# One row of branch B's output weights in three transfers instead of one: a gated pair of attention decodes

## The chip, the core and the metric

The kernel runs on one core of a Trainium2 chip. The metric is the device time of one execution in microseconds; it is taken from several runs, and one execution was profiled beside them. The core has a tensor engine (PE), a vector engine (DVE), a scalar engine (ACT), GpSimd (POOL) and a queue engine (SP, SyncE) that issues most of the transfers. Sixteen DMA engines carry every transfer between HBM and the on-chip buffers.

## The reference

Two branches, A and B, each decode one token for two sequences with 32 heads of 128 over a cache of 4096 tokens. All data are float32.

```python
def branch(x, k_cache, v_cache, wq, wo):          # x: 2 x 1 x 512
    q = (x @ wq).reshape(B, 1, 32, 128).transpose(0, 2, 1, 3)
    scores = einsum("bhqd,bhkd->bhqk", q, k_cache) * 128 ** -0.5
    p = softmax(scores)
    o = einsum("bhqk,bhkd->bhqd", p, v_cache)
    return o.transpose(0, 2, 1, 3).reshape(B, 1, 4096) @ wo     # wo: 4096 x 512

g = sigmoid((A_x * gate_w).sum(-1, keepdims=True))
out = g * branch(A_x, A_k, A_v, A_wq, A_wo) + (1 - g) * branch(A_x, B_k, B_v, B_wq, B_wo)
```

Each of the four caches has 134 MB and each of the four weight matrices 8.4 MB; every byte is read once.

## The kernel before

The work is cut into 32 units: a branch, a group of four heads, and a sequence. A unit's K and its V are 8.4 MB each, laid out as 128 partitions of 64 KB. Three buffers of that size exist: `kt[0]` and `kt[1]` for K in turn, and `vt` for V. DVE multiplies K by the query and sums (L392, L395), takes the maxima, ACT makes the exponentials, and PE multiplies them with V (L371).

SP issues nearly all loads, in the order in which the program is written, and waits before each until its buffer is free. At the end of its list stand the V of the last unit (`load_v(NU - 1)`, into `kt[0]`), branch A's output weights (`load_wo("A")`, into `vt`) and branch B's (`load_wo("B")`, into `kt[1]`, once DVE has read the last K there).

Output weights lie as 128 partitions of 32 rows (`OR` = 32), each row 512 numbers, 2 KB. `load_wo("B")` brings them in seven transfers, each with a semaphore of its own (slots `a`, `b`, `c`, `h`, `i`, `j`, `k`): rows 0 to 15, 16 to 23, 24 to 27 (`EARLY` is 28), 28 and 29, 30, and the two halves of row 31. `load_parts` issues a transfer for each pair of cuts and keeps, in `parts`, what to wait for. PE consumes rows in order: `project_out` multiplies rows 0 to 27 into the accumulator `most` (L466) and waits at the first row of each part; `project_last` multiplies rows 28 to 31 in four strips (L481), with one wait for each part. Between them ACT copies `most` to `kept` (L582), and four small matmuls fold it in (L586). DVE and ACT then copy the four strips to the on-chip totals (L597, L596), and SP and ACT each store one half of the output.

Of the kernel before, what the change touches and what calls it, by code (L numbers as in the profile page):

```python
# [12 lines left out]
P = 128  # L13
# [15 lines left out]
OR = H * DH // P  # L29
DQ = DH // OR  # L30
EARLY = OR - 4
PAD = 72
NP = 2 * NG
SCALE = DH ** -0.5
# [13 lines left out]
class Streams:  # L48
# [32 lines left out]
    def put(self, e, make, reads=(), writes=(), gives=None):  # L81

        self.before(e, reads, writes)
        i = make(self.engines[e])
        if gives is not None:
            i.then_inc(gives, 1)
            return None
        self.ticks[e] += 1
        i.then_inc(self.sems[e], 1)
        point = self.sems[e], self.ticks[e]  # L90
        self.after(point, reads, writes)
        return point
# [51 lines left out]
def tile_gated_decode(ctx: ExitStack, tc: tile.TileContext, ins: dict, out: bass.AP):  # L144
# [12 lines left out]
    slot = small.tile([P, VC], F32, name="slot")  # L157
# [12 lines left out]
    ones = small.tile([P, 1], F32, name="ones")  # L170
    small.tile([P, PAD], F32, name="pad")
    kt = [big.tile([P, NS, DH], F32, name=f"kt{i}") for i in range(2)]
# [9 lines left out]
    with tc.tile_critical():  # L182
        S = Streams(nc, tc)
# [25 lines left out]
        parts = {}  # L209

        def load_parts(item, t, src, slots, *cuts):
            parts[item] = [S.dma("sp", t[:, i:j], src[:, i:j], slot=s) for s, i, j in zip(slots, cuts, cuts[1:])]

        def arrived(e, item, *which):
            p = parts[item]
            S.wait(e, [p[k] for k in which] if which else p)
# [27 lines left out]
        def load_wo(n):  # L244
            t = wo[n]
            src = ins[n + "_wo"].rearrange("(p r) e -> p r e", p=P)
            if n == "A":
                nc.sync.wait_ge(v_free, NU - 1)
                load_parts(("wo", n), t, src, "f", 0, OR)
                return  # L250
            nc.sync.wait_ge(k_free[1], NU // 2)
            load_parts(("wo", n), t, src, "abchi", 0, OR // 2, 3 * OR // 4, EARLY, OR - 2, OR - 1)
            parts["wo", n] += [S.dma("sp", t[:, OR - 1, h], src[:, OR - 1, h], slot=s) for s, h in zip("jk", HALVES)]

        wo = {n: t.rearrange("p r d -> p (r d)").rearrange("p (r e) -> p r e", e=D) for n, t in (("A", vt), ("B", kt[1]))}

# [13 lines left out]
        def vput(e, make, reads=(), writes=(), **kw):  # L270
# [6 lines left out]
                                     slot="y"))  # L277
# [180 lines left out]


        def project_out(k, n, *rows_):  # L460
            bounds = (0,) if n == "A" else (0, OR // 2, 3 * OR // 4)
            for r in range(*rows_):
                if r in bounds:
                    arrived("pe", ("wo", n), bounds.index(r))
                s = r % STRIPS
                put("pe", lambda x: x.matmul(most[s * QT:s * QT + B], on[:, k, r], wo[n][:, r],  # L466
                                             start=n == "A" and r < STRIPS, stop=n == "B" and r >= EARLY - STRIPS),
                    [r_on], [r_most])
# [5 lines left out]
        def strips(*which):  # L474
            for s in which or range(STRIPS):
                yield s, r_acc[s], acc[s][s * QT:s * QT + B, :W], slice(s * W, (s + 1) * W)

        def project_last(part, r, *which):
            arrived("pe", ("wo", "B"), part)
            for _, a, t, e_ in strips(*which):  # L480
                put("pe", lambda x: x.matmul(t, on[:, 1, r], wo["B"][:, r, e_], start=r == EARLY, stop=r == OR - 1), [r_on], [a])  # L481

# [26 lines left out]
        for u in range(2, NU):  # L509
            load_k(u)  # L510
            load_v(u - 1)
        load_v(NU - 1)
        load_wo("A")
        load_wo("B")

        exps(0, 0, 0, lambda make, gives: put("act", make, [r_nm[0], r_sc, r_pad, r_lp, r_nil], [], gives))
# [61 lines left out]
        r_on.writers = [point]  # L578

        project_out(0, "A", OR)  # L580
        project_out(1, "B", EARLY)
        put("act", lambda x: x.activation(kept, most, AF.Copy), [r_most], [r_kept])  # L582
        for r in range(EARLY, OR - 2):
            project_last(3, r)
        for _, a, t, e_ in strips():
            put("pe", lambda x: x.matmul(t, fold, kept[:, e_], start=False, stop=False), [r_fold, r_kept], [a])  # L586
        project_last(4, OR - 2)
        project_last(5, OR - 1, 0, 1)
        project_last(6, OR - 1, 2, 3)

        for h, e in enumerate(("sp", "act")):
            r_total = [R(), R()]
            for i in range(2):
                _, a, t, _ = next(strips(2 * h + i))
# [27 lines left out]
```

## Time and profile before

| | |
|---|---|
| median of 3 runs | 1324.02 us (1323.88 to 1324.05) |
| the profiled execution | 1324.03 us |
| its span, first to last instruction | 1322.2 us |
| DVE busy | 1165.2 us (88%) |
| PE busy | 333.5 us (25%) |
| ACT busy | 100.7 us (8%) |
| DMA | 570.51 MB, mean 431 GB/s over the span |

The profiled execution agrees with the median of the runs. The span is what the trace covers; the rest of the execution lies before the first and after the last instruction. Busy shares are averages over the whole span. The DMA share that the profile gives is the mean over sixteen DMA engines, so a share of 0.125 is two engines at work.

### The profile page before, as it was taken

To read this page: it belongs to the slowest core of one execution; us is meant where nothing else is said; L and a number is where in the kernel's file an instruction comes from. 1 tells how busy PE (TensorE), PEld (TensorE's weight loads), DVE (VectorE), ACT (ScalarE), POOL (GpSimd) and SP (SyncE) were. 2 spreads that over 40 slices of the span, in tenths; PEclk is the share of its full clock that TensorE was granted. 3 is DMA by queue.
4 is the path that set the end of the run, shared out by engine and by line. 5 is a ranking of instruction groups with operands and counts; after the bars stand their busy time and mean duration, and the time that the engine had idled before them with its cause. 6 is when DMAs were issued, how large, how long until landed. Compare 5 with 4: busy or idle time off the path is not lost. (4 is left out here: it accounts for less than half of the span.)

```text
span 1322.2 us, 6170 instructions
## 1 busy us (share of the span) xinstructions
PE 333.5 (25%) x2358; PEld 90.2 (7%) x2358; DVE 1165.2 (88%) x316; ACT 100.7 (8%) x328; POOL 0.7 (0%) x6
## 2 busy tenths in 40 slices
PE   3112223211222221122222122222212232221255
PEld 0000000000000000000000000000000000000011
DVE  1988999999999999999999999999999999999961
ACT  0000100001010000101000010100001010000100
POOL 0000000000000000000000000000000000000000
PEclk9566666556666655666665566666556666655678
DMA  9999999999999999999999999999999999999998
GB/s 406 451 412 443 442 418 442 440 428 432 442 432 426 442 440 418 442 442 416 442 442 418 442 442 428 430 442 434 424 442 442 416 442 442 416 442 442 423 438 350
DMA packets 10820, 570.51 MB, mean 431 GB/s; under 512 B 1207, under 2 KB 1467, under 8 KB 1726
## 3 DMA queue, kind: packets, MB, share of 16 engines
q1 hardware_dynamic: 10804, 570.43, 99.6%
q8 instruction: 3, 0.05, 0.0%
q14 instruction: 3, 0.02, 0.0%
q10 hardware_dynamic: 10, 0.01, 0.0%
HBM read 570.43 MB, written 0.00 MB: 431 GB/s over the span
## 5 line engine op out<-in xcount | busy, mean ns | idle before, releaser
L392 DVE TENSOR_TENSOR kt<-kt,q 128x16384 f32<-128x16384 f32 x31 | 534.0, 17225 | 70.6 <-DVEq L97 70.6
L395 DVE TENSOR_REDUCE sc<-kt 128x128 f32<-128x16384 f32 x31 | 533.8, 17220 | 1.1
L371 PE MATMUL vp<-vt,pr 128*32 128x512 f32 x1984 | 285.0, 739 | 913.5 <-PEq L97 913.5
L371 PEld LDWEIGHTS vp<-vt,pr 128*32 128x32 f32 x1984 | 78.3, 133 | 1120.2 <-issue 1120.2
L367 ACT ACTIVATE pr<-sc,nm 32x128 f32<-32x128 f32 x128 | 50.9, 398 | 107.0 <-ACTq L97 101.7
L430 ACT ACTIVATE pr<-nil 128x512 f32<-128x512 f32 x31 | 19.3, 623 | 457.4 <-ACTq L97 457.4
L451 ACT ACTIVATE vs<-vp,slot 128x128 f32 x15 | 5.5, 367 | 448.6 <-ACTq L97 448.6
L337 PE MATMUL qa<-vt,cols 128*2 128x512 f32 x128 | 19.1, 764 | 39.3 <-PEq L97 39.3
L367 ACT ACTIVATION_READ_ACCUMULATOR pr<-sc,nm (+1 forms) x128 | 23.5, 184 | 0.0
L416 DVE SCALAR_TENSOR_TENSOR vs<-vp,slot,vs 128x128 f32 x45 | 15.8, 351 | 8.6 <-DVEq L97 7.6
L597 DVE COPY kt<-qa 2x128 f32<-2x128 f32 x1 | 0.3, 278 | 23.6 <-PE qa L481 23.6
L352 DVE STREAM_TRANSPOSE vt<-vt 128x1024 f32<-128x1024 f32 x2 | 2.5, 1225 | 17.2 <-ACT vt L348 17.2
L498 DVE TENSOR_REDUCE sc<-kt 128x64 f32<-128x8192 f32 x2 | 17.4, 8686 | 0.1
L496 DVE TENSOR_TENSOR kt<-kt,q 128x8192 f32<-128x8192 f32 x2 | 17.4, 8686 | 0.0
L455 ACT ACTIVATE vp<-nil 128x512 f32<-128x512 f32 x15 | 9.0, 600 | 98.5 <-ACTq L97 98.5
L544 DVE SCALAR_TENSOR_TENSOR vs<-vp,slot,vs 128x128 f32<-128x128 f32 x3 | 1.1, 351 | 13.4 <-ACT vs L542 13.3
L371 PE MATMUL vp<-kt,pr 128*32 128x512 f32 x64 | 9.5, 759 | 10.4 <-DMA kt<-in_B_v_cache_dram 10.4
L400 DVE TENSOR_REDUCE rm<-sc 128x1 f32<-128x128 f32 x31 | 8.7, 281 | 2.3
L406 DVE STREAM_TRANSPOSE q<-qsel 128x128 f32<-128x128 f32 x30 | 9.3, 311 | 1.0
L466 PE MATMUL most<-vt,kt 128*2 128x512 f32 x64 | 8.4, 684 | 6.0 <-DMA vt<-in_A_wo_dram 6.0
L289 DVE COPY cols<-bank 128x8 f32<-128x8 f32 x1 | 0.2, 166 | 10.2 <-PE bank L287 10.2
L401 DVE STREAM_TRANSPOSE across<-rm 128x32 f32<-128x32 f32 x31 | 6.6, 212 | 1.1
(73 smaller groups left out, 56.7 us busy)
## 6 DMA issues: line engine op xcount, KB each, us to landing
kt<-in_A_k_cache_dram SPq DMA_DIRECT2D x2, 4096.0 KB, 35.6
kt<-in_B_wo_dram SPq DMA_DIRECT2D x1, 4096.0 KB, 33.3
kt<-in_B_wo_dram SPq DMA_DIRECT2D x1, 2048.0 KB, 37.7
kt<-in_B_wo_dram SPq DMA_DIRECT2D x1, 1024.0 KB, 39.7
kt<-in_B_wo_dram SPq DMA_DIRECT2D x1, 512.0 KB, 40.5
vt<-in_A_v_cache_dram SPq DMA_DIRECT2D x16, 28.3
kt<-in_B_k_cache_dram SPq DMA_DIRECT2D x16, 42.6
kt<-in_B_wo_dram SPq DMA_DIRECT2D x1, 256.0 KB, 40.6
```

What stands on the lines that cost most here:

```text
L337: last = nc.tensor.matmul(t[h * QT:h * QT + B], cols[:, c], blocks[:, c, i, h], start=c == 0, stop=c == KC - 1)
L367: do(lambda x: x.activation(padded[h, :, b, j * VC:(j + 1) * VC], s[h].rearrange("p (c a) -> p c a", a=VC), AF.Exp, bias=m[h], accum_out=l ...
L371: return x.matmul(vp[c % STRIPS * QT:(c % STRIPS + 1) * QT], padded[:, c].rearrange("p b m -> p (b m)"), t[:, c * VC:(c + 1) * VC].rearran ...
L392: at = D_.do(lambda x: x.tensor_tensor(kt[o], kt[o], q[:, None, :].to_broadcast([P, NS, DH]), op=ALU.mult), after)
L395: at = D_.do(lambda x: x.tensor_reduce(sc[o], kt[o], axis=AX.X, op=ALU.add), at)
L400: at = D_.do(lambda x: x.tensor_reduce(rm, sc[o], axis=AX.X, op=ALU.max), after)
L406: return D_.do(lambda x: x.transpose(q, qsel[:, 0].to_broadcast([P, DH // QT, QT])), at)
L416: at = D_.do(lambda x: x.scalar_tensor_tensor(vs[:, g], vp[:, a * DH:(a + 1) * DH], slot[:, a:a + 1], vs[:, g], op0=ALU.mult, op1=ALU.add) ...
L430: return A_.do(lambda x: x.activation(padded[:, :, b], nil[:, :, None].to_broadcast([P, NVC, G * VC]), AF.Copy))
L455: A_.do(lambda x: x.activation(vp, nil.to_broadcast([P, VC * DH]), AF.Copy))
L496: put("dve", lambda x: x.tensor_tensor(t, t, q[:, None, :].to_broadcast([P, NS // 2, DH]), op=ALU.mult), [r_q], [r])
L498: put("dve", lambda x: x.tensor_reduce(sc[0][:, h * NS // 2:(h + 1) * NS // 2], t, axis=AX.X, op=ALU.add), [r], [R()])
```

## The change

Row 15 (`FEW` = `OR // 2 - 1`) is taken out of the first transfer of branch B's output weights, which now brings rows 0 to 14. Row 15 comes in three transfers of 72, 24 and 32 partitions, issued right behind it and ahead of rows 16 to 23. The three share one semaphore, slot `l`, and PE waits for all of them at row 15. The other transfers stay as they are and in their order.

```diff
+FEW = OR // 2 - 1
+SHARES = (0, 72, 96, P)
...
-            load_parts(("wo", n), t, src, "abchi", 0, OR // 2, 3 * OR // 4, EARLY, OR - 2, OR - 1)
+            load_parts(("wo", n), t, src, "a", 0, FEW)
+            first = parts["wo", n] + [S.dma("sp", t[i:j, FEW], src[i:j, FEW], slot="l") for i, j in zip(SHARES, SHARES[1:])]
+            load_parts(("wo", n), t, src, "bchi", OR // 2, 3 * OR // 4, EARLY, OR - 2, OR - 1)
             parts["wo", n] += [S.dma("sp", t[:, OR - 1, h], src[:, OR - 1, h], slot=s) for s, h in zip("jk", HALVES)]
+            parts["wo", n] = first + parts["wo", n]
...
-            bounds = (0,) if n == "A" else (0, OR // 2, 3 * OR // 4)
+            bounds = {0: 0} if n == "A" else {0: 0, FEW: 3, OR // 2: 4, 3 * OR // 4: 5}
             for r in range(*rows_):
                 if r in bounds:
-                    arrived("pe", ("wo", n), bounds.index(r))
+                    arrived("pe", ("wo", n), bounds[r])
```

The calls of `project_last` name their parts by numbers that are three higher, since three parts stand ahead of them now.

SP's list at the end of the loads, before (`kt_86` is the buffer `kt[1]`, `kt_85` is `kt[0]`; the numbers after a name are partitions and elements):

```order
L106 DMA vt<-in_A_wo_dram 128x16384 [waits v_free]
L106 DMA kt_86<-in_B_wo_dram 128x8192 [waits k_free1]
L106 DMA kt_86<-in_B_wo_dram 128x4096
L106 DMA kt_86<-in_B_wo_dram 128x2048
L106 DMA kt_86<-in_B_wo_dram 128x1024
L106 DMA kt_86<-in_B_wo_dram 128x512
L106 DMA kt_86<-in_B_wo_dram 128x256 x2
```

and now:

```order
L108 DMA vt<-in_A_wo_dram 128x16384 [waits v_free]
L108 DMA kt_86<-in_B_wo_dram 128x7680 [waits k_free1]
L108 DMA kt_86<-in_B_wo_dram 72x512
L108 DMA kt_86<-in_B_wo_dram 24x512
L108 DMA kt_86<-in_B_wo_dram 32x512
L108 DMA kt_86<-in_B_wo_dram 128x4096
L108 DMA kt_86<-in_B_wo_dram 128x2048
```

The first transfer is one row (512 elements) shorter, and three stand between it and the next.

PE's matmuls with branch A's last rows and branch B's rows 0 to 27 (`most` is the accumulator), before:

```order
L466 MATMUL most<-vt,kt_85 2x512 x31
L466 MATMUL most<-kt_86,kt_85 2x512 [waits landed_a]
L466 MATMUL most<-kt_86,kt_85 2x512 x15
L466 MATMUL most<-kt_86,kt_85 2x512 [waits landed_b]
L466 MATMUL most<-kt_86,kt_85 2x512 x7
```

and now:

```order
L471 MATMUL most<-vt,kt_85 2x512 x31
L471 MATMUL most<-kt_86,kt_85 2x512 [waits landed_a]
L471 MATMUL most<-kt_86,kt_85 2x512 x14
L471 MATMUL most<-kt_86,kt_85 2x512 [waits landed_l]
L471 MATMUL most<-kt_86,kt_85 2x512 [waits landed_b]
```

Row 15 has a wait of its own, and PE's order of rows is the same.

More of the change, by code (lines that the diff above doesn't have):

```diff
@@ L583, in tile_gated_decode @@
         for r in range(EARLY, OR - 2):
-            project_last(3, r)
+            project_last(6, r)
         for _, a, t, e_ in strips():
             put("pe", lambda x: x.matmul(t, fold, kept[:, e_], start=False, stop=False), [r_fold, r_kept], [a])
-        project_last(4, OR - 2)
-        project_last(5, OR - 1, 0, 1)
-        project_last(6, OR - 1, 2, 3)
+        project_last(7, OR - 2)
+        project_last(8, OR - 1, 0, 1)
+        project_last(9, OR - 1, 2, 3)
         for h, e in enumerate(("sp", "act")):
```

## The prediction, made before the changed kernel ran

> **What bounds the kernel now.** I read the page first, then the chain that ended last in order of time, then the tail in narrow windows. From the page, the DMA line of the 40 slices and the three totals:
>
> ```profile
> span 1322.2 us, 6170 instructions
> DMA  9999999999999999999999999999999999999998
> DMA packets 10820, 570.51 MB, mean 431 GB/s; under 512 B 1207, under 2 KB 1467, under 8 KB 1726
> q1 hardware_dynamic: 10804, 570.43, 99.6%
> ```
>
> The sixteen DMA engines work in every slice; only the last slice is not full. The span is the time in which 570 MB come in. A change can pay only by fewer bytes, by a higher rate, or by what lies after the moment when not all sixteen engines work any more. This change leaves the bytes alone. The sums below stand against the profiled execution, 1324.03 us, of which 1322.2 is the span and 1.8 lies around it; the median of the runs is 1324.02, the same.
>
> The chain in order of time, its last long piece and what follows:
>
> ```profile
> 1275.71 0.03 issue
> ...
> 1275.79 0.33 SPq L106
> ...
> 1276.16 0.43 SPq L106
> ...
> 1276.63 0.43 SPq L106
> 1277.07 0.04 issue
> 1277.11 40.47 DMA kt<-in_B_wo_dram
> 1317.58 0.04 issue
> ...
> 1319.12 0.27 ACT kt L596
> ```
>
> SP issues the transfers of branch B's output weights as soon as VectorE has left the K buffer (1275.7), and from there on the end is one long transfer. The 40 us are not its own. The timeline of SP and the list of issues show what is queued ahead:
>
> ```profile
> 1237.19 0.33 SPq L106 DMA_DIRECT2D kt<-in_B_v_cache_dram  x1
> 1270.33 0.33 SPq L106 DMA_DIRECT2D vt<-in_A_wo_dram  x1
> 1275.79 3.44 SPq L106 DMA_DIRECT2D kt<-in_B_wo_dram  x7
> 1319.47 0.33 SPq L106 DMA_DIRECT2D out_dram<-kt  x1
> vt<-in_A_wo_dram SPq DMA_DIRECT2D x1, 28.7
> ```
>
> Branch A's output weights land at 1270.33 + 28.7 = 1299.0; B's follow them. So the engines have over 20 us of work queued when B's seven transfers are issued. Next the tail in windows (us, busy time of each engine, granted clock, DMA share, GB/s), after one long window of the steady part:
>
> ```profile
> 200.00:1200.00 1000.00, 239.64 (x1664) 65.82 (x1664) 934.88 (x221) 76.86 (x254) 0.00 (x0) 0.61 1.00 434
> 1316.40:1316.80 0.40, 0.40 (x4) 0.09 (x8) 0.00 (x0) 0.00 (x0) 0.00 (x0) 1.00 1.01 364
> 1316.80:1317.20 0.40, 0.40 (x8) 0.00 (x0) 0.00 (x0) 0.00 (x0) 0.00 (x0) 1.00 0.53 190
> 1317.20:1317.60 0.40, 0.23 (x4) 0.00 (x0) 0.00 (x0) 0.03 (x1) 0.00 (x0) 1.00 0.25 92
> 1317.60:1318.60 1.00, 0.98 (x32) 0.68 (x34) 0.00 (x0) 0.57 (x1) 0.00 (x0) 1.00 0.11 39
> ```
>
> This is the view that decides. The engines do not finish together: all sixteen work until 1316.8, a share of 0.25 (four engines) until 1317.6, and then 0.11 x 16 = 1.8 engine-us are left in one microsecond, that is two engines with about 0.9 us each. A part counts as landed only when its slowest engine is done, so the kernel waits for these two. No view names them.
>
> What hangs on the last landing, from the timeline:
>
> ```profile
> 1318.93 0.09 PEld L481 LDWEIGHTS vp<-kt,kt 128*2 128x2 f32 x2 [0.17 <-DMA kt<-in_B_wo_dram]
> 1319.04 0.27 PE L481 MATMUL bank<-kt,kt 128*2 128x128 f32 x1
> 1319.41 0.27 ACT L596 ACTIVATE kt<-bank 2x128 f32<-2x128 f32 x1
> 1319.77 0.26 ACTq L106 DMA_DIRECT2D out_dram<-kt  x1
> ```
>
> TensorE waits for the last eighth of a row at 1318.93; matmul, copy and store follow in a fixed string. Whatever moves the two last engines moves the end by as much.
>
> **The change part by part.** Row 15 of B's weights (128 partitions x 2 KB) leaves the first transfer and comes in three of its own, of 72, 24 and 32 partitions, between the first transfer and the next. Bytes, source and target stay.
>
> How many engines does a transfer of so many partitions use? The packet counts tell some of it. The kernel before has 75 loads of 128 partitions on q1 (2 query weights, 2 halves of the first K, 31 more K, 32 V, 1 + 7 output weights) and one store of 2 partitions. 75 x (128 + 16) + (2 + 2) = 10804, the count above exactly: one packet for a partition and one small one for each engine that takes part, 16 for 128 partitions and 2 for 2. The other queue fits too:
>
> ```profile
> q10 hardware_dynamic: 10, 0.01, 0.0%
> ```
>
> 2 + 2 (x), 1 + 1 (gate weights), 2 + 2 (second store) is 10. So shares are equal, on as many engines as the partitions allow, up to 16. Taken for 72, 24 and 32 by equal shares this is 12, 12 and 16 engines: twelve engines get 6 + 2 + 2 = 10 rows of 2 KB where they had 8, the other four get 2. That is the whole effect: work goes from four engines to twelve.
>
> [...] This trace shows only counts of 1, 2 and 16.
>
> Price of a 2 KB packet on one engine, in bounds: at the steady rate 434/16 = 27.1 KB per us it is 75 ns; at the rate of the window with the small packets, 364/16 = 22.8, it is 90 ns. That window mixes 1 to 4 KB, so I take 80. What leaves the first transfer is a slice of a longer packet at the steady rate: 8 x 75 = 0.60 us for each engine.
> - A loaded engine: -0.60 + 10 x 0.08 = +0.20 us (0.15 to 0.30).
> - A spared engine: -0.60 + 2 x 0.08 = -0.44 us (-0.45 to -0.42).
>
> Three small semaphore packets more are in the noise of these bounds. The shift happens ahead of the smaller parts, so it holds for every part that follows.
>
> SP issues three transfers more. From the list for this tensor:
>
> ```profile
> L106 SPq DMA_DIRECT2D kt<-in_B_wo_dram x7: 328/430/436, 1275.8 to 1278.8; - x7
> ```
>
> 3 x 0.43 = 1.3 us later for the parts behind row 15, and SP ends at 1280.5 instead of 1279.2. Nothing waits behind it on SP until the store at 1319.47, and the engines reach these parts only after A's weights at 1299.0: cost 0. Without those 18 us of cover it would be up to 1.3.
>
> TensorE waits once more, at row 15, with rows 16 to 31 behind it. Its waits in this stretch:
>
> ```profile
> PE most L466 <- DMA kt<-in_B_wo_dram: 3.4, 3, 1.6
> 1309.11 3.61 PE L466 MATMUL most<-kt,kt 128*2 128x512 f32 x32 [1.59 <-DMA kt<-in_B_wo_dram]
> 1313.95 1.90 PE L466 MATMUL most<-kt,kt 128*2 128x512 f32 x16 [1.23 <-DMA kt<-in_B_wo_dram]
> ```
>
> Sixteen rows take it 3.61 us (0.23 a row) while the engines bring a row in 0.60. It idles before every part, so one wait more in this string costs 0 as long as the 1.2 us of idle before row 16 stand; rows 0 to 14 may begin up to 0.6 us earlier, which nothing uses.
>
> The sum then depends on where the two late engines lie, and the end is the later of them:
> - at least one of them among the twelve: the end moves by 0.0 to +0.2 us. If one is spared, the other ends last and the gap between the two (inside the windows' resolution) is set against +0.2; if none is, the whole +0.2. I take +0.1: 1324.03 + 0.1 = 1324.1 us.
> - both spared: -0.44, and the two are still last, since the third was 0.9 us ahead and comes 0.2 later: 1323.6 us.
>
> [...]
>
> **The rivals.**
> 1. Both late engines are spared, 1323.6. For it: only two are late, and four are spared. Against it: two picked blindly out of sixteen both fall into given four in 4/16 x 3/15 = 5%; engines that are late for one cause may be neighbours, which raises it. I give 0.28.
> 2. The pieces run on fewer engines than equal shares allow, and the kernel is slower. The rows show one engine for one partition and no count between 2 and 16. If 72 and 24 each went to one engine, it would carry 96 + 2 rows where it had 8: -0.60 + 98 x 0.08 = +7.2 us, less up to 1.7 us by which an early engine is ahead (1316.8 against 1318.5), 1329.5 to 1331.3. It passes 0.2% (2.6 us, about what a measurement of this kernel can tell from no change) from two engines down: -0.60 + 50 x 0.08 = +3.4. Against it: the packet counts fit full use everywhere else. 0.03.
> 3. Counts of eight instead of twelve: loaded engines get 9 + 3 + 2 = 14 rows, -0.60 + 14 x 0.08 = +0.5 (0.45 to 0.66), 1324.5. 0.04.
> 4. The change does not do what it says: all pieces over 16 engines. Then each engine has its 8 rows in smaller packets, 8 x 0.005 = +0.04, 1324.1, not to be told from before. 0.03.
>
> **How the numbers follow.** At least one late engine among the twelve has 0.60, with its own range 1324.0 to 1324.3; the four rivals 0.28, 0.03, 0.04 and 0.03; 0.02 for a disturbance that I do not see. The predicted time is 1324.1 us. The range goes down to the spared case less the spread of the runs shown, 1323.6 - 0.2 = 1323.4, and up to the dearer end of eight engines and the same spread, 1324.7 + 0.2 = 1324.9; it leaves out the one-engine case and the unseen. Faster by over 0.2% would take 2.6 us, which no case gives: 0.02. Slower by that much only if pieces run on one or two engines: 0.04. Within 0.2%: 0.94.
>
> **What the changed profile would show.** Packets on q1: 10804 + 128 + 12 + 12 + 16 = 10972 for twelve engines, 10964 for eight, 10976 for sixteen, 10950 for one. DMA issues of B's weights: ten, ending near 1280.5. The windows after 1317: two engines at the end still, their last packet near 1318.1 if both were spared, 1318.5 to 1318.8 otherwise, and the fourteen others 0.2 later. TensorE's last wait ends by as much earlier or later than 1318.93. I would be wrong in kind if the span moved by more than a microsecond, or if the steady part before 1275 did.

## The result, and the profile after

| | before | after |
|---|---|---|
| median of 22 runs each, same chip | 1324.07 us (1323.85 to 1324.55) | 1325.72 us (1324.62 to 1328.05) |
| ratio of the two | | 1.0013 [1.0007, 1.0019] |
| the profiled execution | 1324.03 us, span 1322.2 | 1325.24 us, span 1323.5 |

The changed kernel is 1.65 us slower, which lies outside the predicted range (1323.4 to 1324.9). The difference is within the 0.2% that the prediction called no change, but it is not zero, and there is something else: the runs of the kernel before lie within 0.7 us, those of the changed one are spread over 3.4 us.

The profile after: packet counts and the first queue, from the list of DMA.

```profile
DMA packets 10988, 570.51 MB, mean 431 GB/s; under 512 B 1247, under 2 KB 1507, under 8 KB 1894
q1 hardware_dynamic: 10972, 570.43, 99.7%
```

10972 packets are 168 more than before, 128 + 12 + 12 + 16, as forecast for twelve, twelve and sixteen engines. So the shares are what the prediction said. Bytes and rate over the whole span are unchanged.

The timeline of SP (start, duration, instruction, count):

```profile
1237.82 0.33 SPq L108 DMA_DIRECT2D kt<-in_B_v_cache_dram  x1
1271.74 0.33 SPq L108 DMA_DIRECT2D vt<-in_A_wo_dram  x1
1276.42 10.11 SPq L108 DMA_DIRECT2D kt<-in_B_wo_dram  x10
1320.66 0.28 SPq L108 DMA_DIRECT2D out_dram<-kt  x1
```

Two readings. First, 0.63 us of the longer span are there already when the last V is issued and again when B's weights are (1237.82 against 1237.19, 1276.42 against 1275.79). That is ahead of the change and can't be an effect of row 15's packets; a second profile of the same kernel, below, lacks it. Second, from the start of B's issues to the store it is 1320.66 - 1276.42 = 44.24 us, against 1319.47 - 1275.79 = 43.68 before: +0.56 in the place that was changed.

Where in that place? The list of issues (KB, us from issue to landing of the slowest engine) and the chain, which has the issue times of the first and the next large part:

```profile
kt<-in_B_wo_dram SPq DMA_DIRECT2D x1, 3840.0 KB, 33.7
kt<-in_B_wo_dram SPq DMA_DIRECT2D x1, 2048.0 KB, 37.1
```

```profile
1276.42 0.33 SPq L108
...
1278.03 0.42 SPq L108
```

Rows 0 to 14 land at 1276.42 + 33.7 = 1310.1, rows 16 to 23 at 1278.03 + 37.1 = 1315.1, 5.0 us later. Before, rows 0 to 15 landed at 1309.1 and rows 16 to 23 at 1313.9, 4.8 us for eight rows alone. Row 15, which now stands between the two, costs 0.2 us on whichever engines land last, where a whole row costs 0.6: that fits two rows of it there, not ten. But rows 0 to 14, which are one row fewer, land a microsecond later than sixteen rows did. The windows show the rate while that happens (us, busy time of PE, PEld, DVE, ACT and POOL, granted clock, DMA share, GB/s), first before, then after, two stretches of the tail behind it:

```profile
1307.00:1309.00 2.00, 0.51 (x8) 0.00 (x0) 0.00 (x0) 0.00 (x0) 0.00 (x0) 1.00 0.96 410
```

```profile
1307.00:1309.00 2.00, 1.93 (x20) 0.28 (x12) 0.00 (x0) 0.00 (x0) 0.00 (x0) 1.00 1.10 306
1309.00:1310.00 1.00, 0.00 (x0) 0.00 (x0) 0.00 (x0) 0.00 (x0) 0.00 (x0) 1.00 1.03 358
1310.00:1312.00 2.00, 1.87 (x20) 0.52 (x24) 0.00 (x0) 0.00 (x0) 0.00 (x0) 1.00 0.94 401
...
1318.60:1319.60 1.00, 0.82 (x27) 0.50 (x28) 0.00 (x0) 0.60 (x1) 0.00 (x0) 1.00 0.28 97
```

From 1307 to 1309 the engines are busy (share 1.10), and yet they bring 306 GB/s where 410 stood. This view counts a packet, with all its bytes and its time, in the window in which it starts, so in short windows the rate is best divided by the share: 410/0.96 = 427 GB/s before, 306/1.10 = 278 now. Busy and slow: packets take longer. In the packet records of the trace a 2 KB packet takes 84 ns before; of the 128 packets of row 15, 62 take longer here, up to 168 ns. The 30 KB packets of rows 0 to 14, which are in flight at the same time, take up to 1936 ns where 1138 is the rule, and 41 of the 128 packets of 16 KB behind them take 652 to 1064 ns instead of 611. The tail keeps its form: at the end only a part of the engines is left, a share of 0.28 from 1318.6 on.

### The profile page after: what moved, and what is told of

Read it like the earlier page. It is cut to its first block, busy times and chain, and to the rows that moved or that the text cites. A ratio compares the mean times of both kernels' runs of the same rounds, so it can differ in the third digit from the quotient of the medians.

```text
span 1323.5 us, 6173 instructions
## 1 busy us (share of the span) xinstructions
PE 331.1 (25%) x2358; PEld 89.8 (7%) x2358; DVE 1165.2 (88%) x316; ACT 100.7 (8%) x328; POOL 0.7 (0%) x6
## 3 DMA queue, kind: packets, MB, share of 16 engines
q1 hardware_dynamic: 10972, 570.43, 99.7%
## 5 line engine op out<-in xcount | busy, mean ns | idle before, releaser
L435 ACT ACTIVATE pr<-nil 128x512 f32<-128x512 f32 x31 | 19.3, 624 | 459.3 <-ACTq L99 459.3
## 6 DMA issues: line engine op xcount, KB each, us to landing
kt<-in_B_wo_dram SPq DMA_DIRECT2D x1, 3840.0 KB, 33.7
kt<-in_B_wo_dram SPq DMA_DIRECT2D x1, 2048.0 KB, 37.1
```

What stands on the lines that cost most here:

```text
L435: return A_.do(lambda x: x.activation(padded[:, :, b], nil[:, :, None].to_broadcast([P, NVC, G * VC]), AF.Copy))
```

## The experiments

The theory formed on this, from the rate of 306 GB/s at a share of 1.10 and the packets of up to 168 ns: where a transfer spans only a part of the partitions, the engines that bring it slow one another, which is called crowding below. What they would share no view shows. Rivals: the mere number of transfers costs it (more issues, more completions); the place of the row in the queue does; small packets do; the longer execution is chance.

**The same kernel again, and row 15 in other cuts.** Four kernels on one chip; 33 runs of the kernel before on it have a median of 1324.15 us. The numbers of the parts that PE waits for follow the number of transfers in every kernel; those lines are left out of the edits below.

The changed kernel once more, without an edit:

> The changed kernel once more, for a second profile. In the first one the 2 KB packets of row 15 took up to 168 ns instead of 84 and the tenth transfer took SP 5.9 us to issue. Theory C (crowding: the sixteen engines work on few partitions at a time and slow one another): most engines again lose about 1 us more in row 15 than their share says, and the time is 1.0 to 2.5 us above the kernel before. Theory N (number of transfers queued: the late tenth issue costs the time): the long issue is there again, and its length goes with the time. Theory S (work is only shifted between engines, as predicted; the rest was a chance of the runs): 1323.6 to 1324.3 us.

1326.28 us (1324.42 to 1327.44), ratio 1.0014 [1.0005, 1.0023]; the profiled execution is the fastest of its eleven runs, 1324.42. Its rows of the SP timeline, of the list of issues, and its window:

```profile
1275.64 10.21 SPq L108 DMA_DIRECT2D kt<-in_B_wo_dram  x10
1319.84 0.28 SPq L108 DMA_DIRECT2D out_dram<-kt  x1
```

```profile
kt<-in_B_wo_dram SPq DMA_DIRECT2D x1, 3840.0 KB, 33.6
```

```profile
1307.00:1309.00 2.00, 1.48 (x16) 0.19 (x8) 0.00 (x0) 0.00 (x0) 0.00 (x0) 1.00 0.99 289
```

1319.84 - 1275.64 = 44.20 us from the first issue to the store, 0.52 more than before: the same as in the first profile (0.56), without its earlier 0.63. The drop in the rate is there again. So about half a microsecond in the changed place is shown in two profiles; it is not chance.

Row 15 as one transfer of 128 partitions:

```diff
-SHARES = (0, 72, 96, P)
+SHARES = (0, P)
```

> Row 15 in one transfer of 128 partitions, still apart from rows 0 to 14. Undoes the split by partitions alone; eight transfers where the kernel before has seven. C: no engine crowding, within 0.3 us of the kernel before. S: the same, since nothing is shifted. N: eight issues, one more than before, well under the ten that were slow: no change, or a small part of the loss.

1324.15 us (1323.79 to 1324.38), ratio 1.0 [0.9991, 1.0009]. The same three views:

```profile
1275.79 10.74 SPq L108 DMA_DIRECT2D kt<-in_B_wo_dram  x8
1319.34 0.33 SPq L108 DMA_DIRECT2D out_dram<-kt  x1
```

```profile
kt<-in_B_wo_dram SPq DMA_DIRECT2D x1, 3840.0 KB, 32.5
```

```profile
1307.00:1309.00 2.00, 1.94 (x24) 0.31 (x16) 0.00 (x0) 0.00 (x0) 0.00 (x0) 1.00 1.07 451
```

The 2 KB packets keep their 84 ns and the 30 KB packets their 1138, but for one of 1605 beside a 16 KB packet of the queue that the profile calls instruction (before, the 32 KB packet beside it took 1681 instead of 1213). Rows 0 to 14 land 32.5 us after their issue, 1.1 to 1.2 us sooner than ahead of the three pieces. A row of its own, its place, its 2 KB packets and its wait on PE cost nothing.

Row 15 in two transfers of 64 partitions, and in three transfers that each have all 128 partitions and a part of the columns:

```diff
-SHARES = (0, 72, 96, P)
+SHARES = (0, 64, P)
```

> Row 15 in two transfers of 64 partitions: every engine still gets 8 rows of 2 KB (4 and 4), nine transfers. S: no engine is loaded or spared, so no change, 1324.1 us. C: each half crowds all sixteen engines on half of the partitions, so row 15 costs every engine about 1.2 us instead of 0.6, and the end comes 0.5 to 0.7 us later, with no relief for the late engines. N: between the kernels with eight and ten transfers.

```diff
-SHARES = (0, 72, 96, P)
+SHARES = (0, 192, 320, D)
...
-t[i:j, FEW], src[i:j, FEW]
+t[:, FEW, i:j], src[:, FEW, i:j]
```

> Row 15 in three transfers of all 128 partitions, cut by columns (768, 512 and 768 bytes a partition). As many transfers as the changed kernel, ten, and equal shares. N: as slow as the changed kernel, +1.0 to +2.5 us, and a long tenth issue. C: no crowding, only smaller packets: 16 more on each engine, +0.1 us or so by the 15 ns that a 2 KB packet at most pays over its bytes. S: the same +0.1.

Halves: 1325.98 us (1325.07 to 1326.71), ratio 1.0013 [1.0004, 1.0022]. Columns: 1324.24 us (1324.07 to 1324.58), ratio 1.0 [0.9991, 1.0009]. Of the halves the packet count and the first issue from the list of DMA, and the window; then the SP timeline and the window of the columns:

```profile
q1 hardware_dynamic: 10964, 570.43, 99.6%
kt<-in_B_wo_dram SPq DMA_DIRECT2D x1, 3840.0 KB, 34.1
```

```profile
1307.00:1309.00 2.00, 2.00 (x20) 0.28 (x12) 0.00 (x0) 0.00 (x0) 0.00 (x0) 1.00 1.21 312
```

```profile
1276.24 29.53 SPq L108 DMA_DIRECT2D kt<-in_B_wo_dram  x10
```

```profile
1307.00:1309.00 2.00, 1.67 (x20) 0.27 (x16) 0.00 (x0) 0.00 (x0) 0.00 (x0) 1.00 1.14 454
```

This pair decides between number and cut. Three transfers with smaller packets cost nothing (454 GB/s); two transfers with full-sized packets cost as much as the change, though they load every engine evenly (10964 = 10804 + 2 x (64 + 16), sixteen engines each, four rows twice, eight in all as before). What they share with the change is that a transfer spans a part of the partitions. SP is occupied for 29.53 us with the ten issues of the columns, and the time doesn't move: the cover that the prediction named for SP's issues holds far beyond 1.3 us.

**The same cuts where they are large.** The V of the last unit is 8.4 MB, 64 KB for a partition; cut in the same ways, on the kernel before, the rate can be read directly. 27 runs of the kernel before on the same chip have a median of 1324.19 us.

```diff
-load_parts(("v", u), kt[0], tokens("_v_cache", u), "g", 0, NS)
+parts["v", u] = [S.dma("sp", kt[0][i:j], tokens("_v_cache", u)[i:j], slot=s)
+                 for s, i, j in zip("gm", (0, 64, 128), (64, 128))]
```

(two waits follow instead of one; shortened). The rival has the same two transfers, `kt[0][:, i:j]`, cut by columns.

> The kernel before, with one other change: the V of the last unit (8.4 MB, 64 KB a partition) comes in two transfers of 64 partitions instead of one of 128. Row 15's suspected cost, 32 times as large and away from small packets. Every engine still brings 8 packets of 64 KB. Theory C (engines crowd on half of the partitions, and the two halves go at half the rate): 8.4 MB take 38.6 us instead of 19.3, so up to +19 us; less where the two halves overlap, over +12 in any case. Theory K (only small packets, or the few bytes at each change of transfer, cost something): under +1 us.

> Control to the kernel with V in two halves: the same V in two transfers of all 128 partitions, 32 KB a partition each. C and K both: within 0.5 us of the kernel before. A third theory, that two transfers where one was cost the time by themselves, would show here as in the other.

Halves 1346.6 us, ratio 1.017 [1.0151, 1.0189]; columns 1324.15 us, ratio 1.0001 [0.9991, 1.0011]. Windows over the last V, halves and then columns:

```profile
1260.00:1275.00 15.00, 9.91 (x64) 2.69 (x64) 15.00 (x1) 0.63 (x1) 0.00 (x0) 0.73 1.03 210
1275.00:1295.00 20.00, 0.00 (x0) 0.00 (x0) 1.30 (x4) 1.96 (x8) 0.00 (x0) 0.50 1.00 207
```

```profile
1275.00:1295.00 20.00, 12.07 (x80) 3.79 (x80) 4.18 (x14) 2.92 (x10) 0.00 (x0) 0.72 0.99 428
```

With a share of 1.0, every engine busy, a transfer to 64 partitions moves 207 to 210 GB/s, half of 428. The engines aren't idle: a 64 KB packet takes 5.1 us instead of 2.42. What the packets wait for no view shows. The cost of the two halves is +22.4 us for 8.4 MB.

Two sharper cuts of the same V, on a chip on which 21 runs of the kernel before have a median of 1324.17 us: (0, 32, 96, 128), whose middle piece has 64 partitions as a half has, but others, and the cuts of the change itself, (0, 72, 96, 128).

> The last unit's V in three transfers, of partitions 0 to 31, 32 to 95 and 96 to 127; each uses all sixteen engines, with 2, 4 and 2 partitions each. The two halves of 64 ran at 210 GB/s where 435 is usual. What is it about the halves? [...] Theory H (a transfer of 64 or fewer partitions, or of half of a block of HBM, is slow whatever its partitions): all three at 210 GB/s or less, +20 us or more. [...]

> The changed kernel's three pieces on the last unit's V, 32 times the bytes of row 15. Theory S (only shares are shifted): twelve engines bring 10 packets of 64 KB instead of 8, 24.1 us instead of 19.3, +4.8 us at the end. [...]

Against theory H stands that it matters which partitions they are. With the middle piece at the usual 435 GB/s (9.7 us) and the outer two at the 210 GB/s of the halves (10.0 us each), an estimate from these rates is 29.7 us for 19.3, +10.4.

The first took 1339.26 us (+15.1), ratio 1.0115 [1.0097, 1.0134]. Its windows, one in each piece:

```profile
1262.00:1268.00 6.00, 5.22 (x32) 1.52 (x36) 6.00 (x1) 0.00 (x0) 0.00 (x0) 0.60 0.85 175
1272.00:1279.00 7.00, 0.00 (x0) 0.00 (x0) 4.92 (x4) 2.29 (x8) 0.00 (x0) 0.86 1.03 440
1282.00:1290.00 8.00, 0.00 (x0) 0.00 (x0) 0.00 (x0) 0.00 (x0) 0.00 (x0) 0.50 0.82 181
```

64 partitions move 440 GB/s if they are 32 to 95, and 210 if they are 0 to 63. That is which partitions, not how many, and it rules out any theory by size. The pieces of 32 ran at half the rate: their packets of some 5 us are almost as long as these windows, and by share they have 175/0.85 = 206 and 181/0.82 = 221 GB/s. The total came between this estimate and theory H's +20, at least in part by one engine that lags: its last packet of this V ends at 1294.9, 3.1 us after that of the next one.

The cuts of the change took 1365.22 us (+41), ratio 1.0311 [1.0292, 1.033], far over theory S's +4.8, and over the +22.4 of the two halves.

```profile
1262.00:1286.00 24.00, 8.64 (x64) 2.23 (x56) 14.30 (x4) 2.59 (x9) 0.00 (x0) 0.71 0.99 208
1303.00:1315.00 12.00, 0.00 (x0) 0.00 (x0) 0.00 (x0) 0.00 (x0) 0.00 (x0) 0.50 0.77 98
1325.00:1332.00 7.00, 6.11 (x48) 1.55 (x40) 0.35 (x1) 0.37 (x1) 0.00 (x0) 0.86 1.02 440
```

208 GB/s, then 98 at a share of 0.77, which is 127 with all engines busy. A 64 KB packet took up to 8.4 us instead of 2.4. The spared engines had gone on to branch A's weights by then, and their packets there slowed too: no 64 KB packet that started from 1290 to 1303 took under 7.2 us. So an engine that carries nothing of a piece is slowed as well. Why the rate falls as low as 127 GB/s isn't settled.

**Row 15 away from its place.** On the chip of the two V halves, row 15 is issued by ACT's queue instead of SP's as soon as the buffer is free, so that its packets come between the long ones of other transfers; once in the three pieces, once whole.

```diff
+        def load_row15():
+            src = ins["B_wo"].rearrange("(p r) e -> p r e", p=P)
+            nc.scalar.wait_ge(k_free[1], NU // 2)
+            parts["wo", "B"][1:1] = [S.dma("act", wo["B"][i:j, FEW], src[i:j, FEW], slot="l") for i, j in zip(SHARES, SHARES[1:])]
...
         act_second(NP - 1, last=True)
+        load_row15()
```

(shortened)

> The changed kernel's pieces of 72, 24 and 32 partitions, but issued from ACT's queue at the same moment (ACT is idle there), so that each engine takes them between the long packets of SP's queue instead of one behind the other. The engines' shares stay: twelve get 10 rows, four get 2. C: the crowding is spread over long packets and mostly goes; the relief of the late engines stays, -0.4 us, so 1323.6 to 1324.0, under the kernel before. If the loss were one of shares (twelve loaded engines set the end), it would stay at +1.0 to +2.0.

> Control: row 15 in one transfer of 128 partitions from ACT's queue. No shift of shares and no crowding: the kernel before within 0.3 us. Against it stands the kernel with pieces on ACT's queue; the difference of the two is what sparing four engines by 12 KB each brings by itself: -0.4 us if both late engines are among the four, +0.2 if neither is.

Pieces 1326.04 us (1325.23 to 1326.84), ratio 1.0015 [1.0006, 1.0024]; whole 1324.3 us, ratio 1.0002 [0.9993, 1.0011]. I had expected the pieces to be faster by 0.4, with the crowding thinned out and the relief kept; they lose as much as the change. Windows of both, pieces first:

```profile
1283.00:1303.00 20.00, 9.83 (x80) 3.01 (x76) 3.71 (x17) 0.96 (x2) 0.00 (x0) 0.76 1.00 399
```

```profile
1283.00:1303.00 20.00, 11.62 (x84) 3.33 (x80) 3.71 (x17) 0.96 (x2) 0.00 (x0) 0.76 0.99 425
```

(425 - 399) x 20 us are 0.52 MB, 1.2 us at 428 GB/s, most of the 1.74 between the medians: that is what 256 KB of row 15 cost when they are strewn among packets of 64 KB, which took 2.58 us in the median from 1283 to 1297 instead of 2.42. Thinning doesn't remove the crowding, it spreads it.

**Which engines are late, and is their relief worth anything?** Five kernels load only partitions 32 to 32 + N of rows 14 and 15 in one transfer (32 to 95 took in 440 GB/s above), so that some engines carry nothing there. They leave work out: the other partitions of these rows never arrive.

```diff
-FEW = OR // 2 - 1
-SHARES = (0, 72, 96, P)
+FEW = OR // 2 - 2
+SHARES = (32, 32 + N)
...
-t[i:j, FEW], src[i:j, FEW]
+t[i:j, FEW:OR // 2], src[i:j, FEW:OR // 2]
```

> Leaves work out: of rows 14 and 15 only partitions 32 to 79 are loaded (48 partitions, 12 engines with 4 rows of 4 KB each; four engines bring nothing). Here engines are spared without anyone taking over their bytes. Against the kernel with 64 partitions, which spares no one more than another, it shows whether the late engines are among the four that the changed kernel spares: if both are, the end comes another 0.6 us earlier (4 packets of 155 ns), about 1.2 us before the kernel before, 1322.9; if one is or none is, both kernels end alike, 0.6 us before the kernel before, 1323.5.

> Control to the kernel with 48 partitions; leaves work out: of rows 14 and 15 only partitions 32 to 95 are loaded (64 partitions, all sixteen engines with 4 rows of 4 KB instead of 8). Every engine has 0.6 us less to do: 1323.5 us. [...]

> Leaves work out: of rows 14 and 15 only partitions 32 to 75 are loaded, 44 partitions. If shares are equal on the largest count up to 16, eleven engines get 4 rows of 4 KB and five get none (10860 packets on q1), and no share crosses a border of four partitions, so nobody is crowded. Against the kernel with 64 partitions (1323.63 us): if both late engines are among the five, another 0.4 to 0.6 us earlier, 1323.0 to 1323.2; if one or none is, the same 1323.6.

> The same with partitions 32 to 83, 52 partitions: thirteen engines with 4 rows, three with none (10870 packets). If both late engines are among the last three, 1323.0 to 1323.2, otherwise 1323.6. A rival by which any transfer on fewer than sixteen engines slows the others: over 1324 us, as the kernel with 48 partitions.

> The same with partitions 32 to 91, 60 partitions: fifteen engines with 4 rows, one with none (10880 packets). One engine alone can't be both late ones: 1323.4 to 1323.6, and at the end of the profile one engine instead of two is left alone if the spared one was late.

| N | us (range) | less the kernel before | packets on q1 less 10804 | engines |
|---|---|---|---|---|
| 64 | 1323.63 (1323.34 to 1323.76) | -0.54 | 80 = 64 + 16 | 16 |
| 60 | 1323.51 (1323.35 to 1324.17) | -0.62 | 75 = 60 + 15 | 15 |
| 52 | 1323.56 (1323.26 to 1324.14) | -0.57 | 65 = 52 + 13 | 13 |
| 48 | 1324.44 (1324.14 to 1326.13) | +0.27 | 64 = 48 + 16 | 16 |
| 44 | 1323.31 (1323.04 to 1323.71) | -0.82 | 55 = 44 + 11 | 11 |

64 and 48 ran on one chip (the kernel before: 1324.17 us), 60, 52 and 44 on another (1324.13).

The counts, from the lists of DMA for 64, 48 and 44, and a window of 48 and of 44:

```profile
q1 hardware_dynamic: 10884, 570.17, 99.7%
```

```profile
q1 hardware_dynamic: 10868, 570.10, 99.6%
```

```profile
1306.50:1308.50 2.00, 1.99 (x20) 0.28 (x12) 0.00 (x0) 0.00 (x0) 0.00 (x0) 1.00 0.95 309
```

```profile
q1 hardware_dynamic: 10859, 570.09, 99.7%
```

```profile
1306.50:1308.50 2.00, 2.00 (x24) 0.47 (x20) 0.00 (x0) 0.00 (x0) 0.00 (x0) 1.00 1.06 453
```

The expectations for 44, 52 and 60 are one packet too high, an error of my sums; 11, 13 and 15 engines are the expected numbers. For 48 I had expected twelve engines; it is sixteen with three partitions each. In every size counted alone here (11 engines for 44, 16 for 48, 13 for 52, 15 for 60, 16 for 64 and 128) the count is the largest up to sixteen that divides the partitions; of 72, 24 and 32 the sum alone is counted, 40, and 12 + 12 + 16 fits it.

48 became the cleanest test of crowding by accident. It moves 64 KB less than 64 and takes 0.8 us longer, at 309 GB/s where 44 has 453 in the same window. Its shares are of three partitions; 44, 52, 60 and 64 have shares of four, and their times show none of it. The expectation for 44 speaks of a border every four partitions; no run shows one, the runs show these two sizes of share, from partition 32 on. 44 and 52, a little smaller and a little larger from the same start, also speak against a limit that lies in the addresses in HBM.

In 44, 52, 60 and 64 an engine carries four partitions of two rows, or nothing; only the number of spared engines differs, five, three, one and none. Against the kernel before on the same chip 60 and 52 gain as much as 64 to within 0.1 us, and 44 gains some 0.2 more. By the times alone this is thin: the ranges overlap, and the intervals of the ratios of 44 and 64, 0.9994 [0.9985, 1.0003] and 0.9997 [0.9988, 1.0006], don't part them.

The packet records of the traces settle it. They name no engine, but on an engine a packet starts some 4 ns before the recorded end of the one ahead of it, so that the packets can be strung into sixteen sequences. In the kernel before, fourteen of them end by 1317.63 and two at 1318.34 and 1318.55. These two have one thing in common: each also carried a packet of the queue that the profile calls instruction,

```profile
q8 instruction: 3, 0.05, 0.0%
```

16 KB at 104.4 us the one, at 1300.0 us the other (the third comes when the loads are over). The one at 1300.0 took 0.96 us, and the 32 KB packet behind it 1.68 instead of 1.21, 1.43 us in all, which the engine doesn't make up before the end. The other engine ends every large transfer from that packet on, over 1150 us, 1.3 to 1.5 us after the middle of the sixteen, where it lay within 0.1 us of it before. So the two late engines are late by one packet each of the instruction queue. In the changed kernel the engines with these two packets carry two packets of row 15 each, not ten: both are spared, and one of them still ends last. With 44 partitions both are spared, with 52 only the one of 1300, so that the other ends last, and with 60 neither; in the table 44 alone gains. In the profiles the relief is as large as its packets: from the end of branch A's weights to their own end the two take 18.38 and 19.80 us with 44 partitions, and 19.00 and 20.42 with 64. Why the medians show only some 0.2 of these 0.62 us is open; the profiled execution of 44 was behind by 0.4 us ahead of that place.

None of the kernels that load everything beat the kernel before.

## Why the prediction was wrong

- **The end is the last landing of two late engines: right.** In the windows of the changed kernel too only a few engines are left at the end, and the store follows them.
- **Shares of 12, 12 and 16 engines: right,** by the count of 10972. That the same four engines are spared by the pieces of 72 and of 24, as the 10 and 2 rows of the sum have it, nothing before shows; strung into engines, the records of the changed kernel fit best with ten packets of row 15 on twelve engines and two on four.
- **What row 15 does to the packets of the other transfers: this is the term that failed; the sum has none.** It took the price of a 2 KB packet, 80 ns, from whole transfers of 128 partitions (84 ns in the records), and put it on pieces of a part of the partitions, whose packets took up to 168 ns; and it let all other packets go on as before. Strung into engines, the records show what came instead. On the engine that ends last, a spared one, the last two 30 KB packets of rows 0 to 14 took 1.30 and 1.94 us instead of 1.14 each, +0.96 (second profile: 1.27 and 1.88, +0.87). Then the relief came, just as priced: its two packets of row 15 took 0.20 us where eight take 0.64 with row 15 whole, -0.44. The 16 KB packets behind added 0.1. Together this is +0.6 and +0.5, the +0.56 and +0.52 of the SP timelines.
- **"Loaded +0.20, spared -0.44":** the difference of the two is right, both levels are wrong. From the end of A's weights to its own end an engine takes 19.6 us with row 15 whole. In the changed kernel the loaded ones take 20.6 to 20.8, about +1.0, and the two spared ones that aren't late 20.0 to 20.2, about +0.4. The 0.6 between them is the work that was shifted; on top of it all engines lost 0.8 to 1.0 us, most of it not in row 15 (its packets take 108 to 110 ns in the mean) but in the 30 KB and 16 KB packets around it.
- **Which engines: the forecast put at least one late engine among the twelve. Both are spared, which is rival 1,** given 0.28; the case of one loaded and one spared is out with it. Rival 1's 1323.6 us did not come, because the spared engines were held up by more than their relief. The small plus of the forecast has the sign of the result by luck: a loaded engine's longer share, from which it was taken, doesn't set the end.
- **Rivals 2, 3 and 4** are out by the packet count. Rival 2 had the right sign with the wrong cause: no engine is missing in the count; the packets took longer, 108 to 110 ns in the mean for row 15 instead of 84. (For three pieces over sixteen engines each the count would be 10804 + 128 + 48 = 10980, not the 10976 of the prediction.)
- **SP's three issues cost 0: right, with a wrong duration.** 3 x 0.43 was forecast, ending at 1280.5; it was 10.11 us for ten, ending at 1286.5, and 29.53 us in the columns, all of it hidden.
- **PE's added wait costs 0: right.** The whole row 15 has the same wait and the time of before.
- **"Wrong in kind if the span moved by more than a microsecond, or if the steady part before 1275 did":** both happened in the first profile, 1.3 us, of which 0.63 ahead of the change. The second profile moved by 0.4 and had none of the early part.

What stays open is the rest of the median. The profiled executions explain half a microsecond in the changed place; the medians are 1.65 and 2.1 us over before, and single runs from 0.3 to 4.0. All kernels with crowding are spread (1.6 us in the halves, 1.6 in the pieces on ACT's queue, 3.0 and 3.4 in the two series of the change), and those without are not (0.6 in row 15 whole, 0.5 in columns). In the halves, where no engine is relieved, the profile has 1321.75 - 1276.23 = 45.52 us from the first issue to the store, 1.84 over before, so crowding alone can cost that much. That in the change its size depends on how the engines happen to stand to each other when the pieces come is a guess; no run controlled it.

Why a part of the partitions crowds is not shown: no view tells what the packets wait for, and the runs show only which cuts crowd and by how much. A cut that keeps the relief and avoids the crowd wasn't found, and was not tried further; whether there is one is not shown.

## What to carry to other kernels

Cut a load by columns or rows of each partition, not by partitions: here two halves of the partitions used all engines and still ran at half the rate (207 to 210 GB/s, 428 by columns), and the pieces slowed their neighbours in the queue (partitions 32 to 95 in shares of four are the exception here, 440 GB/s). Before a packet is priced, ask whether the row that it is priced from has the same engines going to the same partitions; count the engines, look apart from that at which partitions a transfer spans, and ask what the moved bytes do to the packets around them. Where a tail hangs on two engines, ask first what made them late: here it was a 16 KB packet of the instruction queue on each. Moving bytes to the others can win at most their lead, 0.9 us in the profile before, and here the crowd cost more than the 0.44 us that was moved.

## What the runs showed of the hardware

- 64 partitions take in 440 GB/s if they are 32 to 95, and 207 to 210 if they are 0 to 63 or 64 to 127, with all sixteen engines busy in each.
- The two DMA engines that end last are those that carried a 16 KB packet of the instruction queue (0.96 us, and 1.68 instead of 1.21 us for the packet behind it). The engines never idle in between (a share of 1.00 from 200 to 1200 us), so nothing evens this out: the engine that carried its packet at 104.4 us is 1.46 us behind the middle of the sixteen at 120 us and 1.32 at 1279.
- Sixteen shares of three partitions take 0.8 us longer in two rows than sixteen of four (48 against 64 partitions, both from 32 on, with fewer bytes).
- Crowding passes over to packets of other transfers, on the same queue (30 KB: 1138 to 1936 ns) and from another queue (64 KB: 2.42 to 2.58 us in the median), and in a large load the rate goes down to 127 GB/s with all engines busy, under a third of 428.
- With over 20 us of transfers queued, a single issue on SP can take long. The group of B's weights in the changed kernel, by tile (minimum, mean as given, and longest in ns):

```profile
L108 SPq DMA_DIRECT2D kt<-in_B_wo_dram x10: 320/426/5851, 1276.4 to 1280.7; - x10
```

The tenth issue took 5.85 us, in the columns one took 13.0. What it waits for no view shows; it was hidden in every kernel here, and wouldn't be if a short transfer that someone needs stood behind it.
